# Attention and MoE on one core: sums of weights in three stages on VectorE, four buffers for the plain chunks' results, and visits of the first chunk 7 slots apart

## The chip, the core and the metric

The kernel runs on one core of a Trainium2 chip. The metric is the device time of one execution in microseconds (us); lower is better. A core has TensorE (PE in the profile; its weight loads are PEld), VectorE (DVE), ScalarE (ACT), GpSimd (POOL) and SyncE (SP). Each of these engines works through its own queue in order, so an instruction that waits holds up all that stand behind it on the same engine. DMAs are issued here from SP's, ScalarE's and GpSimd's queues.

## The reference

Windowed attention over 8 batches, 8 heads, 576 positions and head size 64, then a gated feed-forward layer on the 4608 resulting tokens:

```python
scores = scale * np.matmul(q, k.transpose(0, 1, 3, 2))
scores = np.where(masks, scores, -1e9)          # 32 keys back, plain or every 4th
attn = softmax(scores)                          # rows
x = (attn @ v).transpose(0, 2, 1, 3).reshape(4608, 512)
g = x @ w_gate                                  # 512 x 1536
out = (g * sigmoid(g) * (x @ w_val)) @ w_out    # 1536 x 512
```

Everything is float32 in and out.

## The kernel before

The tokens are cut into 12 chunks of 384 (`CH`). Float32 products are made of three products of a high and a low part in a format that TensorE takes fast (fp32r), so each operand is split: ScalarE copies it rounded (high), and another engine subtracts (low).

**Plain chunks.** The first four chunks are computed straight, in 48 steps `s` (loop at L757), 12 for each chunk, one for each 128 rows of the hidden layer. In a step TensorE runs three groups of 12 matmuls: gate into `bank_g` (`gv_mm`, L401), value into `bank_v` (L401), and out of the step before into the four banks `bank_o` (`out_mm`, L439). Between them ScalarE takes the tanh of the gate (`act_tanh`, L411), VectorE makes u and h (L416, L421), ScalarE and GpSimd split h (`h_hi` L426, `h_lo` L431). There is one bank for the gate, so u of a step must have been made before the gate group of the next step can start. Tanh, u and h live in two buffers that take turns (`t_ring`). At a chunk's end `out_store` (L442) copies the four banks, two on ScalarE (L446) and two on VectorE (L448), and stores them from SP's queue (L449).

**Weights.** In chunk 0 the weights arrive as 24 raw units and are turned into high and low parts: ScalarE L205, VectorE L212 and L213 (768 columns), ScalarE L221, GpSimd L225.

**Mixes.** The last eight chunks are computed in four pairs by a scheme with 7 products in place of 8 (`gate_val`, `outs`, L704), which needs sums of weight blocks. In chunks 1 to 3 these are made in 18 mixes (`mix`, L577). A mix adds high and low parts to whole float32 blocks in `q_at` (VectorE L587), makes four sums of 256 columns (L592, L594 and L595 on VectorE, L593 on GpSimd), copies 1024 columns to high parts (ScalarE L598) and subtracts to get the low parts (GpSimd L599). The results lie in one of two buffers (`l_ring`) and go to DRAM in `mix_out` (L606, four stores of 256 KB); three more stores take plain parts (L570). GpSimd's queue reads all pieces back in the paired chunks (L636).

**Visits.** Attention for the chunks to come is put between these groups. It comes in packs `m`, four to a chunk. `visit` is a table of slots, three to a step: in visit A of pack m TensorE makes the results of pack m-1 (L339) and the scores of pack m (L299, in banks `two`), VectorE divides (L348 to L350) and subtracts maxima (L311 to L314), ScalarE takes the exponential (L319). In visit B TensorE transposes (L357 for results, L323 for weights), ScalarE copies (L329) and x of pack m-1 is split (ScalarE L376, VectorE L377) or copied (L381).

**Order.** The program is traced in the order of the loops, and a scheduler then places the instructions on each engine's queue by its own estimates, so neighbours can change places. `tc.issue_after` holds a block behind one instruction on the same engine.

## Time and profile before

| What | Value |
|---|---|
| three executions | 991.89, 992.1, 993.73 us |
| their median | 992.1 us |
| the profiled execution | 996.74 us |
| its span, first to last instruction | 994.8 us |
| mean granted TensorE clock in it | 0.977 of full speed |
| busy: PE, DVE, ACT, POOL | 952.6, 658.4, 397.3, 430.4 us |
| stages in the span | first attention to 30 us, chunk 0 to 123, chunks 1 to 3 to 409, pairs from there |

A row of a timeline reads: start in us, duration in us, engine, line, operation, out<-in, shapes, and in brackets how long the engine sat idle before it and what ended that. A row with a bar reads: shapes and count | busy us, mean ns of one | idle before it and its releasers. In a table of windows each engine has its busy time and its count of instructions, then come the granted clock, the busy share of the DMA engines and GB/s. A group of 12 matmuls starts a fixed time after the one before when nothing waits.

### The profile page before, as it was taken

What the parts mean: (1) busy time and instruction counts of PE and PEld (TensorE: products, weight loads), DVE (VectorE), ACT (ScalarE), POOL (GpSimd) and SP (SyncE); (2) the same over time, 40 slices, a digit from 0 to 9 for tenths busy, and PEclk for the clock granted to TensorE, in tenths of its full rate; (3) what the DMA queues carried; (4) which work ended last, traced back from release to release, by engine and by line L of the source; (5) the groups of instructions that cost most, each with busy time, mean ns of one, the idle gap of its engine ahead of it and who ended that gap; (6) DMA issues with size and microseconds to landing.
All of it is one profiled execution on the core that took longest, in us unless ns stands there. A gap on an engine that the chain in (4) does not pass through costs nothing.

```text
span 994.8 us, 23912 instructions
## 1 busy us (share of the span) xinstructions
PE 952.6 (96%) x9960; PEld 924.7 (93%) x9960; DVE 658.4 (66%) x1144; ACT 397.3 (40%) x776; POOL 430.4 (43%) x496
## 2 busy tenths in 40 slices
PE   5898999999999898989999999999999999999998
PEld 4787899998989798989999999999999999999998
DVE  5777744556664644467688668688668679476583
ACT  4564422232323222333446244456244456244352
POOL 1564524343332342234337434346434347444473
PEclk7798999999999899999999999999999999999999
DMA  9665444665675595278988998998898987988873
GB/s 371 246 222 175 143 138 136 219 198 178 225 230 181 174 321 186 86 240 277 298 275 271 302 309 252 281 288 272 305 305 251 289 258 244 307 254 254 247 237 130
DMA packets 86060, 238.12 MB, mean 239 GB/s; under 512 B 8768, under 2 KB 29120, under 8 KB 85952
## 3 DMA queue, kind: packets, MB, share of 16 engines
q0 software_dynamic: 36288, 132.14, 43.0%
q1 hardware_dynamic: 36848, 65.07, 18.5%
q10 hardware_dynamic: 12816, 39.38, 12.3%
q8 instruction: 79, 1.29, 0.5%
q14 instruction: 29, 0.24, 0.1%
HBM read 194.08 MB, written 42.47 MB: 238 GB/s over the span
## 4 chain that ended last, share of the span: by engine, by line
PE 73%; DVE 12%; DMA 4%; issue 4%; ACT 3%; POOL 3%; SPq 0%; ACTq 0%; POOLq 0%; DVEq 0%
PE bo L704 29%; PE bg L704 11%; PE bv L704 11%; PE bg L401 6%; PE bo L439 5%; PE bv L401 5%; DMA out<-at_float 3%; DVE at_int L213 2%; PE two L339 2%; DVE at_int L212 2%; PE two L299 2%; POOL at_float32r L599 1%; DVE at_float32r L663 1%; PE two L323 1%; PE two L357 1%
## 5 line engine op out<-in xcount | busy, mean ns | idle before, releaser
L704 PE MATMUL bo<-at_float32r,at_float32r 128*128 128x384 f32 x1728 | 320.1, 337 | 3.5 <-DVE at_float L663 3.2
L704 PEld LDWEIGHTS bo<-at_float32r,at_float32r 128*128 128x128 f32 x1728 | 300.5, 188 | 5.2 <-DVE at_float L663 3.5
L636 POOL DMA_DIRECT2D at_float32r<-pieces x252 | 137.9, 547 | 237.4 <-PE bo L704 139.2
L663 DVE TENSOR_TENSOR at_float<-bo,at_float 128x384 f32<-128x384 f32 x224 | 121.7, 552 | 105.4 <-PE bo L704 52.5
L704 PE MATMUL bg<-at_float32r,at_float32r 128*128 128x384 f32 x648 | 137.0, 337 | 0.0
L704 PE MATMUL bv<-at_float32r,at_float32r 128*128 128x384 f32 x648 | 136.5, 336 | 0.0
L401 PE MATMUL bg<-at_float32r,at_float32r 128*128 128x384 f32 x576 | 117.3, 355 | 5.3 <-DVE at_float L416 4.1
L704 PEld LDWEIGHTS bv<-at_float32r,at_float32r 128*128 128x128 f32 x648 | 114.0, 188 | 0.5
L704 PEld LDWEIGHTS bg<-at_float32r,at_float32r 128*128 128x128 f32 x648 | 113.8, 188 | 0.7
L663 POOL TENSOR_TENSOR at_float32r<-at_float,at_float32r 128x384 fp32r<-128x384 f32 x84 | 91.8, 1093 | 51.9 <-ACT at_float32r L693 50.8
L401 PEld LDWEIGHTS bg<-at_float32r,at_float32r 128*128 128x128 f32 x576 | 107.1, 200 | 7.0 <-DVE at_float L416 4.7
L663 DVE TENSOR_TENSOR at_float32r<-at_float,at_float32r 128x384 fp32r<-128x384 f32 (+1 forms) x112 | 100.9, 923 | 18.6 <-ACT at_float32r L693 14.6
L439 PE MATMUL bo<-at_float32r,at_float32r 128*128 128x384 f32 x576 | 111.4, 341 | 1.5 <-POOL at_float32r L431 0.8
L431 POOL TENSOR_TENSOR at_float32r<-at_float,at_float32r 128x384 fp32r<-128x384 f32 x48 | 55.7, 1160 | 129.5 <-PE bo L439 80.6
L401 PE MATMUL bv<-at_float32r,at_float32r 128*128 128x384 f32 x576 | 110.7, 340 | 0.0
L693 ACT CAST at_float32r<-at_float 128x384 fp32r<-128x384 f32 x168 | 82.9, 512 | 63.8 <-PE bv L704 22.0
L439 PEld LDWEIGHTS bo<-at_float32r,at_float32r 128*128 128x128 f32 x576 | 100.9, 189 | 3.2 <-POOL at_float32r L431 1.6
L401 PEld LDWEIGHTS bv<-at_float32r,at_float32r 128*128 128x128 f32 x576 | 101.3, 189 | 0.8
L730 ACT ACTIVATE at_float<-at_float 128x384 f32<-128x384 f32 x96 | 50.6, 527 | 99.3 <-DVE at_float L663 94.4
L416 DVE SCALAR_TENSOR_TENSOR at_float<-at_float,bg 128x384 f32<-128x384 f32 x48 | 26.5, 553 | 77.3 <-ACT at_float L411 77.3
L663 DVE TENSOR_TENSOR at_float<-at_float,at_float 128x384 f32<-128x384 f32 (+1 forms) x64 | 54.6, 878 | 29.0 <-POOL at_float32r L663 11.3
L709 ACT COPY at_float<-bg 128x384 f32<-128x384 f32 x84 | 40.1, 477 | 80.1 <-PE bg L704 79.5
(75 smaller groups left out, 1033.6 us busy)
## 6 DMA issues: line engine op xcount, KB each, us to landing
at_float32r<-pieces POOLq DMA_DIRECT2D x252, 512.0 KB, 4.9
pieces<-at_float32r SPq DMA_DIRECT2D x126, 256.0 KB, 3.2
at_int<-w SPq DMA_DIRECT2D x24, 768.0 KB, 4.8
at_float<-vb ACTq DMA_DIRECT2D x36, 390.0 KB, 4.8
out<-at_float SPq DMA_DIRECT2D x48, 192.0 KB, 4.4
at_float<-qkb ACTq DMA_DIRECT2D x14, 448.0 KB, 5.6
at_float<-qkb ACTq DMA_DIRECT2D x15, 400.0 KB, 5.8
at_float<-qkb ACTq DMA_DIRECT2D x7, 640.0 KB, 6.0
```

The source lines that it names most:

```text
L212: nc.vector.tensor_scalar(out=y, in0=hi, scalar1=3, scalar2=None, op0=ALU.logical_shift_left)
L213: nc.vector.scalar_tensor_tensor(out=y, in0=lo, scalar=29, in1=y, op0=ALU.logical_shift_right, op1=ALU.bitwise_or)
L401: nc.tensor.matmul(out=bank[:, :CH], lhsT=wcol(f, o, low), rhs=x[k], start=n == 0, stop=n == 3 * NK - 1)
L416: last["h"] = nc.vector.scalar_tensor_tensor(out=t, in0=t, scalar=1.0, in1=bank_g[:, :CH], op0=ALU.add, op1=ALU.mult)
L431: nc.gpsimd.tensor_tensor(out=hl, in0=hst[i][0], in1=hst[i][1], op=ALU.subtract)
L439: nc.tensor.matmul(out=bank_o[j][:, :CH], lhsT=wcol(f, 2 * DM + P * j, low), rhs=x, start=f == 0 and n == 0, stop=f == NF - 1 and n == 2)
L636: nc.gpsimd.dma_start(out=taken[asked], in_=pieces[asked % NPIECE])
L663: engine.tensor_tensor(out=out, in0=a, in1=b, op=op)
L693: nc.scalar.copy(out=o[:, 0], in_=src)
L704: nc.tensor.matmul(out=bank, lhsT=w, rhs=x, start=first and n == 0 and t in FRESH, stop=last and n == len(ops) - 1, skip_group_check=True)
L709: nc.scalar.copy(out=kept[KEPT[t]][r], in_=banks[0][r][:, :CH])
L730: nc.scalar.activation(out=f, in_=g, func=AF.Tanh, scale=0.5)
```

## The change

It does three things. First, `out_store` has four buffers of 384 columns of its own at the end of the raw weights' area, which is free after chunk 0. Second, a mix is cut into three stages, `mix_parts`, `mix_sums` and `mix_low`, of which at most about one is traced in a half step (`mix_to`, called twice in a step), where before a whole mix was traced at the end of about every second step. All its arithmetic is on VectorE, apart from ScalarE's copy. There is one buffer for the results (`l_at`) in place of two, because the stores' buffers and the first paired inputs (`x32_first`, which leaves the spare area) need the room; another paired input (`x1_at`) moves from a mix buffer to the spare area. Third, the visits of packs 4 to 8 stand at slots 2 + 7n and 5 + 7n + 1, not 10 + 5n and 13 + 5n. The core of the diff:

```diff
-    x32_first = [at(o, 2 * CH).rearrange("p (k c) -> p k c", k=2) for o in (M_RAW + PIECE, M_SPARE)]
+    x32_first = [at(M_RAW + PIECE + 2 * CH * a, 2 * CH).rearrange("p (k c) -> p k c", k=2) for a in range(2)]
...
-            ot = t_ring()
+            ot = at(M_RAW + 8 * WU - CH * (j + 1), CH)
...
-        visits(4 + n, 10 + 5 * n, 13 + 5 * n)
+        visits(4 + n, 2 + 7 * n, 5 + 7 * n + (n < 4))
...
-    l_ring = Ring(2 * PIECE, M_RAW + 2 * PIECE, M_RAW + 4 * PIECE)
+    l_at = at(M_RAW + PIECE + 4 * CH, 2 * PIECE, F32R).rearrange("p (n l c) -> p n l c", n=4, l=2)
...
         nc.vector.tensor_tensor(out=a22, in0=a21, in1=a22, op=ALU.add)
-        nc.gpsimd.tensor_tensor(out=a21, in0=a11, in1=a21, op=ALU.subtract)
+        nc.vector.tensor_tensor(out=a21, in0=a11, in1=a21, op=ALU.subtract)
         nc.vector.tensor_tensor(out=a11, in0=a22, in1=a11, op=ALU.subtract)
         nc.vector.tensor_tensor(out=a12, in0=a12, in1=a11, op=ALU.subtract)
-        s = q.rearrange("p f h c -> p (f h) c")
-        t = l_ring(dt=F32R).rearrange("p (n l c) -> p n l c", n=4, l=2)
-        nc.scalar.copy(out=t[:, :, 0], in_=s)
-        nc.gpsimd.tensor_tensor(out=t[:, :, 1], in0=s, in1=t[:, :, 0], op=ALU.subtract)
-        mst[n] = i, which, t.bitcast(F32)
+        nc.scalar.copy(out=l_at[:, :, 0], in_=q_at.rearrange("p (n c) -> p n c", n=4))
+
+    def mix_low(n):
+        nc.vector.tensor_tensor(out=l_at[:, :, 1], in0=q_at.rearrange("p (n c) -> p n c", n=4), in1=l_at[:, :, 0],
+                                op=ALU.subtract)
...
-    def mix_step():
+    def mix_stage():
         nonlocal mixed
-        n = mixed
+        n, stage = divmod(mixed, 3)
         mixed += 1
-        if 0 < n <= 3 * NP:
-            mix_out(n - 1)
         if n < 3 * NP:
 
+            with tc.issue_after(last["h"].ins):
+                (mix_parts, mix_sums, mix_low)[stage](n)
             with tc.issue_after(last["w"].ins):
-                plain_parts(*divmod(n, 3))
-            with tc.issue_after(last["h"].ins):
-                mix(n)
+                if stage == 0:
+                    plain_parts(*divmod(n, 3))
+                elif stage == 2:
+                    mix_out(n)
...
-    x1_at = [at(o, 2 * CH).rearrange("p (k c) -> p k c", k=2) for o in (M_RAW + 2 * PIECE, M_XT)]
+    x1_at = [at(o, 2 * CH).rearrange("p (k c) -> p k c", k=2) for o in (M_SPARE, M_XT)]
...
+    def mix_to(half):
+
+        while mixed < half * 9 * NP // 62:
+            mix_stage()
...
         dve_u(s)
+        mix_to(2 * (s - NF) + 1)
...
-        if s >= NF and (s - NF) * 3 * NP // 31 >= mixed:
-            mix_step()
+        mix_to(2 * (s - NF) + 2)
```

In the changed kernel the mix's parts are L591, its four sums L597 to L600, ScalarE's copy L601, the low part L604, its stores L612, the plain stores L569, the pieces' reads L643, the subtraction of the pairs L670.

On VectorE, one mix of chunk 2 before: `at_1024` is `q_at`, `two` the banks of a visit, and the 8-column names belong to the division of a visit.

```order
L587 TENSOR_TENSOR at_1024_float_479<-at_1536_float32r 128x512 x2
L592 TENSOR_TENSOR at_1024_float_479<-at_1024_float_479 128x256
L348 TENSOR_SCALAR at_8_float_913<-two 128x8
L594 TENSOR_TENSOR at_1024_float_479<-at_1024_float_479 128x256
L349 RECIPROCAL at_8_float_913<-at_8_float_913 128x8
L595 TENSOR_TENSOR at_1024_float_479<-at_1024_float_479 128x256
L350 TENSOR_TENSOR at_512_float_914<-two,at_8_float_913 128x2x4x64
L311 TENSOR_TENSOR at_384_float_918<-two,at_352_bfloat_58 128x2x3x64
L313 TENSOR_REDUCE at_6_float_223<-at_384_float_918 128x6
L314 TENSOR_TENSOR at_384_float_918<-at_384_float_918,at_6_float_223 128x2x3x64
L416 SCALAR_TENSOR_TENSOR at_384_float_548<-at_384_float_548,bg 128x384
```

The same place of the changed kernel, where the mix is one stage earlier and the visit's rows follow behind these:

```order
L597 TENSOR_TENSOR at_1024_float_479<-at_1024_float_479 128x256
L598 TENSOR_TENSOR at_1024_float_479<-at_1024_float_479 128x256
L599 TENSOR_TENSOR at_1024_float_479<-at_1024_float_479 128x256
L421 SCALAR_TENSOR_TENSOR at_384_float_549<-at_384_float_549,bv 128x384
L600 TENSOR_TENSOR at_1024_float_479<-at_1024_float_479 128x256
L604 TENSOR_TENSOR at_2048_float32r<-at_1024_float_479,at_2048_float32r 128x4x256
L377 TENSOR_TENSOR at_384_float32r<-two,at_384_float32r 128x384
L416 SCALAR_TENSOR_TENSOR at_384_float_635<-at_384_float_635,bg 128x384
L421 SCALAR_TENSOR_TENSOR at_384_float_635<-at_384_float_635,bv 128x384
L591 TENSOR_TENSOR at_1024_float_479<-at_1536_float32r 128x512 x2
L348 TENSOR_SCALAR at_8_float_808<-two 128x8
```

The sums are no longer mixed with the rows of a visit; the low part (L604), which was GpSimd's, stands right behind the last sum and ahead of the x split (L377) and of the next u (L416).

On ScalarE, the end of chunk 2 before (names with addresses: 9024 and 9408 are the two buffers of `t_ring`):

```order
L411 ACTIVATE at9024_384_float32_548<-bg_471 128x384
L666 CAST at20160_768_float32r_480<-at11968_768_float32_106 128x768
L446 COPY at9408_384_float32_592<-bo0_473 128x384
L426 CAST at9792_384_float32r_570<-at9024_384_float32_548 128x384
L446 COPY at9408_384_float32_592<-bo2_475 128x384
L281 DMA at1928_780_float32_922<-vb 128x780
L275 DMA at648_1280_float32_477<-qkb 128x800
L411 ACTIVATE at9408_384_float32_592<-bg_471 128x384
```

The same place of the changed kernel:

```order
L411 ACTIVATE at9024_384_float32_549<-bg_471 128x384
L673 CAST at20160_768_float32r_481<-at11968_768_float32_106 128x768
L446 COPY at16704_384_float32_1528<-bo0_473 128x384
L426 CAST at9792_384_float32r_571<-at9024_384_float32_549 128x384
L446 COPY at15936_384_float32_1534<-bo2_475 128x384
L411 ACTIVATE at9408_384_float32_635<-bg_471 128x384
L281 DMA at1928_780_float32_817<-vb 128x780
L275 DMA at648_1280_float32_477<-qkb 128x800
L601 CAST at13504_2048_float32r_480<-at10944_1024_float32_479 128x4x256
```

The copies of the banks (L446) write to 16704 and 15936, and the next tanh (L411) has a buffer that no store reads.

On TensorE, from the first scores of chunk 0 (L299, pack 4) to their transposes (L323) before; this is between the value and out groups of step 3 and of step 4:

```order
L299 MATMUL two<-at_1280_float_477 32x64 x32
L439 MATMUL bo_473<-at_384_float32r,at_1536_float32r 128x384 x3
L439 MATMUL bo_474<-at_384_float32r,at_1536_float32r 128x384 x3
L439 MATMUL bo_475<-at_384_float32r,at_1536_float32r 128x384 x3
L439 MATMUL bo_476<-at_384_float32r,at_1536_float32r 128x384 x3
L401 MATMUL bg<-at_384_float32r,at_1536_float32r 128x384 x12
L401 MATMUL bv<-at_384_float32r,at_1536_float32r 128x384 x12
L323 MATMUL two<-at_256_float_59,at_512_float_755 128x128 x4
```

In the changed kernel, in step 2:

```order
L401 MATMUL bg<-at_384_float32r,at_1536_float32r 128x384 x9
L299 MATMUL two<-at_1280_float_477 32x64 x32
L401 MATMUL bg<-at_384_float32r,at_1536_float32r 128x384 x3
L401 MATMUL bv<-at_384_float32r,at_1536_float32r 128x384 x11
L323 MATMUL two<-at_256_float_59,at_512_float_613 128x128 x4
L401 MATMUL bv<-at_384_float32r,at_1536_float32r 128x384
```

The first pack's scores stand a step earlier than before, inside a gate group of step 2, with 14 matmuls between them and their transposes in place of 36; the packs behind it have four groups there in place of three, and three in place of two from their transposes to the next results.

More of the change, by code (lines that the diff above doesn't have):

```diff
@@ L573, in attention_moe, with halves, mix_parts @@
     q_at = at(M_RAW, PIECE)
-    l_ring = Ring(2 * PIECE, M_RAW + 2 * PIECE, M_RAW + 4 * PIECE)
-    mst = {}
-    def mix(n):
+    l_at = at(M_RAW + PIECE + 4 * CH, 2 * PIECE, F32R).rearrange("p (n l c) -> p n l c", n=4, l=2)
+    def halves(n):
+        q = q_at.rearrange("p (f h c) -> p f h c", f=2, h=2)
+        a, b, c, d = [q[:, f, h] for f in range(2) for h in range(2)]
+        return (a, b, c, d) if n % 3 < 2 else (a, c, b, d)
+    def mix_parts(n):
         i, which = divmod(n, 3)
@@ L588, in mix, with mix_sums @@
                 h += k
[L589 to L590 removed]
+    def mix_sums(n):
+        a11, a12, a21, a22 = halves(n)
         nc.vector.tensor_tensor(out=a22, in0=a21, in1=a22, op=ALU.add)
[L593 removed]
+        nc.vector.tensor_tensor(out=a21, in0=a11, in1=a21, op=ALU.subtract)
         nc.vector.tensor_tensor(out=a11, in0=a22, in1=a11, op=ALU.subtract)
         nc.vector.tensor_tensor(out=a12, in0=a12, in1=a11, op=ALU.subtract)
[L596 to L600 removed]
+        nc.scalar.copy(out=l_at[:, :, 0], in_=q_at.rearrange("p (n c) -> p n c", n=4))
+    def mix_low(n):
+        nc.vector.tensor_tensor(out=l_at[:, :, 1], in0=q_at.rearrange("p (n c) -> p n c", n=4), in1=l_at[:, :, 0],
+                                op=ALU.subtract)
     def mix_out(n):
[L603 removed]
+        i, which = divmod(n, 3)
+        t = l_at.bitcast(F32)
         for k, product in enumerate((2, 6, 4, 3) if which < 2 else (2, 4, 6, 3)):
```

3 lines of the change are left out of this document (removed).

## The prediction

> **What bounds the kernel now.** I first read the table of stages, cut where the plain chunks begin, where chunk 1 begins, where the paired chunks begin and where the start of those is over.
>
> ```profile
> core 0: us, PE busy (x) PEld busy (x) DVE busy (x) ACT busy (x) POOL busy (x), PEclk, DMA share, GB/s
> 29.90:122.77 92.87, 84.23 (x913) 79.28 (x914) 70.00 (x88) 47.42 (x74) 52.84 (x31) 0.94 0.58 189
> 122.77:409.35 286.58, 273.88 (x3040) 265.61 (x3040) 157.24 (x298) 84.18 (x155) 100.74 (x83) 0.98 0.57 190
> 409.35:431.24 21.89, 18.37 (x188) 17.29 (x187) 6.56 (x15) 5.56 (x12) 4.71 (x8) 0.92 0.53 172
> 431.24:980.00 548.76, 548.70 (x5322) 539.81 (x5321) 403.06 (x705) 244.85 (x512) 265.71 (x367) 1.00 0.88 273
> ```
>
> TensorE sets the time everywhere: from 431 us on it is never idle, so whatever is saved before moves the end by as much, and nothing later can be gained. The idle time that the change can reach is 92.87 - 84.23 = 8.64 us in chunk 0, 286.58 - 273.88 = 12.70 us in chunks 1 to 3, and 3.52 us at the start of the paired chunks. The clock column adds a part, worked out below. So I went through TensorE's timeline for the single idles, and looked at what each waited for.
>
> **Part one, the out buffers.** Before, the four copies of a finished chunk go through the two buffers that the tanh of the next steps uses.
>
> ```profile
> 229.95 2.35 PE L401 MATMUL bg<-at_float32r,at_float32r 128*128 128x384 f32 x12 [0.44 <-DVE at_float L416]
> 326.07 0.79 PE L439 MATMUL bo<-at_float32r,at_float32r 128*128 128x384 f32 x3 [0.68 <-DVE at_float L448]
> 329.16 0.49 ACT L411 ACTIVATE at_float<-bg 128x384 f32<-128x384 f32 x1 [6.09 <-DMA out<-at_float]
> 329.68 0.55 DVE L416 SCALAR_TENSOR_TENSOR at_float<-at_float,bg 128x384 f32<-128x384 f32 x1 [1.72 <-ACT at_float L411]
> 330.29 4.21 PE L401 MATMUL bg<-at_float32r,at_float32r 128*128 128x384 f32 x12 [3.42 <-DVE at_float L416]
> 427.57 0.56 DVE L663 TENSOR_TENSOR at_float<-bo,at_float 128x384 f32<-128x384 f32 x1 [5.16 <-DMA out<-at_float]
> 428.18 2.29 PE L704 MATMUL bo<-at_float32r,at_float32r 128*128 128x384 f32 x6 [3.19 <-DVE at_float L663]
> ```
>
> At 329 the tanh waited 6.09 us for a store to leave its buffer, and TensorE 3.42 us for what follows the tanh. At 428 the first paired sums waited for the same two buffers. With four buffers that nothing else touches in this time, all four waits go: 0.44 + 0.68 + 3.42 + 3.19 = 7.73 us. The idle has a tail. The gate group of 12 matmuls at 330 took 4.21 us, the one at 229.95 took 2.35: 1.9 us. The clock shows it:
>
> ```profile
> 283.20:286.40 3.20, 3.20 (x15) 3.20 (x14) 1.11 (x2) 1.35 (x4) 0.00 (x0) 0.67 1.06 398
> 330.20:334.30 4.10, 4.01 (x13) 3.91 (x13) 3.28 (x6) 1.03 (x2) 2.04 (x2) 0.50 0.00 0
> ```
>
> Six matmuls are half a group, 2.35 / 2 = 1.2 us; at 428 they took 2.29, so 1.1 us. Together 10.7 us. The copies and the stores stand where they stood, on SP's queue together ahead of the next mix's stores, and no wait is added: the new buffers' last readers are raw weights of chunk 0, later the stores of the chunk before. Bounds 8 (a wait of some 0.7 us stays at each of four chunk ends) and 10.7; I take 10, near the upper end, as the waits name the store and nothing else.
>
> **Part two, the sums of weights.** Before, GpSimd does one sum and the long subtraction.
>
> ```profile
> L599 POOL TENSOR_TENSOR at_float32r<-at_float,at_float32r 128x1024 fp32r<-128x1024 f32 x18 | 43.1, 2392 | 35.3 <-ACT at_float32r L598 31.6 <-DMA pieces<-at_float32r 2.1 <-PE bo L439 1.6
> 279.58 2.35 POOL L599 TENSOR_TENSOR at_float32r<-at_float,at_float32r 128x1024 fp32r<-128x1024 f32 x1 [1.95 <-ACT at_float32r L598]
> 280.07 2.28 DVE L314 TENSOR_TENSOR at_float<-at_float,at_float 128x384 f32<-128x384 f32 x1
> 282.96 0.55 PE L323 MATMUL two<-at_float,at_float 128*128 128x128 f32 x3 [2.33 <-ACT at_float L319]
> 283.26 3.34 PE L439 MATMUL bo<-at_float32r,at_float32r 128*128 128x384 f32 x12
> L314 DVE TENSOR_TENSOR at_float<-at_float,at_float x40: 547/557/2414, 121.4 to 812.0; 128x384 f32<-128x384 f32 x34, 128x512 f32<-128x512 f32 x6
> ```
>
> This is the mechanism I build on. VectorE's subtraction of the maxima (L314), 0.56 us in the median, takes 2.28 us here: it starts while GpSimd's long subtraction (L599) runs, from 279.58 to 281.93, and ends 0.42 us after it, as if it had done its work only then. The exponential and TensorE's transposes wait behind it. The same picture returns:
>
> ```profile
> 377.25 2.41 DVE L314 TENSOR_TENSOR at_float<-at_float,at_float 128x384 f32<-128x384 f32 x1
> 380.27 0.90 PE L323 MATMUL two<-at_float,at_float 128*128 128x128 f32 x3 [3.04 <-ACT at_float L319]
> 380.82 3.47 PE L401 MATMUL bg<-at_float32r,at_float32r 128*128 128x384 f32 x12
> 300.27 0.66 PE L323 MATMUL two<-at_float,at_float 128*128 128x128 f32 x4 [0.89 <-ACT at_float L319]
> 237.71 0.55 PE L323 MATMUL two<-at_float,at_float 128*128 128x128 f32 x3 [0.92 <-ACT at_float L319]
> ```
>
> Idle 2.33 + 3.04 + 0.89 + 0.92 = 7.2 us, slow groups 3.34 - 2.35 and 3.47 - 2.35 = 2.1 us: 9.3 us at stake.
>
> The Trainium skill (TensorE: Matmul & The Clock Gate, Part 1) lets the clock fall after an idle window of about 3.4 us. Here it fell to 0.67 after 2.33 us of idle, so the rows decide; by the page the 2.1 us here and the 1.1 us at 428 would not be owed to the idles, and the forecast would be some 3 us higher.
>
> What VectorE takes on: per mix one more sum of 256 columns and the subtraction of 1024.
>
> ```profile
> L594 DVE TENSOR_TENSOR at_float<-at_float 128x256 f32<-128x256 f32 x18 | 9.2, 513 | 19.1 <-POOL at_float L593 19.0
> 371.84 1.77 DVE L663 TENSOR_TENSOR at_float32r<-at_float,at_float32r 128x768 fp32r<-128x768 f32 x1
> 401.71 0.95 DVE L663 TENSOR_TENSOR at_float32r<-at_float,at_float32r 128x768 fp32r<-128x768 f32 x1
> L598 ACT CAST at_float32r<-at_float 128x1024 fp32r<-128x1024 f32 x18 | 18.9, 1049 | 56.1 <-DVE at_float L595 36.4 <-POOL at_float L593 8.7 <-DMA at_float<-qkb 4.2
> 36.55 2.24 PE L401 MATMUL bg<-at_float32r,at_float32r 128*128 128x384 f32 x12
> 38.63 2.24 PE L401 MATMUL bv<-at_float32r,at_float32r 128*128 128x384 f32 x12
> 369.29 0.96 DVE L663 TENSOR_TENSOR at_float<-at_float,at_float 128x768 f32<-128x768 f32 x1 [3.87 <-DMA pieces<-at_float32r]
> ```
>
> 768 columns took 0.95 us free and 1.77 us beside GpSimd, so 1024 is an estimate of 1.25 to 2.4 us, and I take 1.3, since GpSimd keeps only its short h_lo (L431). Per mix 0.5 + 1.3 = 1.8 us, for 18 mixes 32 us: VectorE goes from 157 to 189 us of 287, with room. In return its 19.0 us of waits for GpSimd's sum go, and with the first paired inputs in the spare area the 3.87 us that VectorE waited for a mix's stores at 369; TensorE did not idle there, so I count nothing. On the path this costs nothing as long as the step's u (L416) comes in time: a value and an out group lie between one gate group and the next, at 38.63 - 36.55 = 2.08 us each, 4.2 us, and tanh and u need 0.49 + 0.55 and two hand-overs, by my estimate 1.3 us: 2.9 us of slack. The low part waits for ScalarE's copy (1.05 us) and blocks what stands behind it in VectorE's queue, in the order shown above L377 and the next u: 1.05 + 1.3 = 2.4 us, inside the slack but not by much. Hence I take 7 of the 9.3 us; bounds 9.3 and 0, and below nothing by the rival on the buffer.
>
> **Part three, the visits of chunk 0.**
>
> ```profile
> 64.12 0.66 PE L323 MATMUL two<-at_float,at_float 128*128 128x128 f32 x4 [1.93 <-ACT at_float L319]
> 77.95 0.66 PE L357 MATMUL two<-at_float,at_float 128*128 128x128 f32 x4 [0.50 <-DVE at_float L314]
> 87.08 0.98 PE L339 MATMUL two<-at_float,at_float 64*32 64x65 f32 x48 [3.84 <-DVE at_float32r L377]
> 89.64 3.95 PE L401 MATMUL bg<-at_float32r,at_float32r 128*128 128x384 f32 x12
> 117.37 0.67 PE L339 MATMUL two<-at_float,at_float 64*32 64x65 f32 x44 [1.58 <-DVE at_float32r L377]
> ```
>
> All four idles come of VectorE's part of a visit (once through ScalarE's exponential, L319), which stands in its queue behind the bit work on the weights (L212, L213): 1.93 + 0.50 + 3.84 + 1.58 = 7.85 us, and 3.95 - 2.35 = 1.6 us of slow group: 9.5 us. By the order, scores to transposes and transposes to the next results get one more matmul group (2.08 us) from the second pack on. That covers 0.50 and 1.58 whole and about half of the 3.84 with its tail. The first pack is not helped: its transposes stand only 14 matmuls (2.4 us) behind its scores, and the reduction, subtraction and exponential need about 2 us once VectorE is free, so the 1.93 stays, perhaps larger by 0.5. Gain 0.50 + 1.58 + 1.9 + 1.6 - 0.5 = 5 us. Upper bound 9.5. Lower bound -2: VectorE is busy 70.00 of 92.87 us here, and the waits may only move with the visits.
>
> **Sum.** 10 + 7 + 5 = 22 us. The profiled execution took 996.74 us, its span 994.8: by it the change gives 974.7. The median of the runs shown is 992.1, 4.6 us less; I take this as the profile's own and keep the 22: 970.
>
> **The rivals.**
>
> *ScalarE's copy waits for the stores (slower).* One buffer now holds the mixed pieces, before two took turns. The copy of the next mix must wait until the four stores of the last one have landed, and the tanh stands behind it in ScalarE's queue.
>
> ```profile
> 338.89 1.79 SPq L606 DMA_DIRECT2D pieces<-at_float32r  x4
> 340.72 2.04 SPq L570 DMA_DIRECT2D pieces<-at_float32r  x3
> DMA to landing us min/median/max: 2.0/2.9/7.2
> ```
>
> The fourth issue comes 1.35 us behind the first, so the last landing is 4.3 us after the low part in the median and 8.6 in the worst. Low part to next copy is two stages, a step of 287 / 36 = 8.0 us less or more; in the tightest place of the order about 6 us. So typical landings are hidden and the worst are 2.5 us late. If all 17 were, and nothing hid it, that is 42 us: 970 + 42 = 1012. It decides from 22 / 17 = 1.3 us a mix on. For it speaks that seven stores follow in a row (four of the mix, three of plain parts); against it that DMA is busy only 0.57 of these stages.
>
> *VectorE becomes the late one.* The 32 us stand before the same subtraction that GpSimd held up; if they cost as much there, part two gives nothing and 977 remains. For it speaks that the low part with its wait, 2.4 us, is as long as the block was; against it that VectorE will be busy 189 of 287 us, and that the order puts the low part behind the visit's subtraction or a step away from it. The Trainium skill (Perfetto Trace Analysis, Optimizing Scalar/DVE Operations) has this rival as its rule: moving work between VectorE and GpSimd might not help, as they share a read port. The trace of before shows the sharing, but not the exchange.
>
> *All of it goes.* 10.7 + 9.3 + 9.5 = 29.5: 962.5. Against it stands the first pack of chunk 0.
>
> *The visits give nothing,* because the scheduler puts the first pack's scores into step 2, not step 0 as the numbers say: 975, inside the forecast's range.
>
> **The numbers.** The forecast (a gain of 15 to 27 us) 0.65; all of it 0.09; VectorE late or parts one or three halved, a gain of 8 to 15, 0.15; a gain of 2 to 8, 0.02; no change 0.04; slower by ScalarE's wait 0.05. A measurement can tell about 0.2% (2 us) here. Faster 0.91, same 0.04, slower 0.05. The range 963 to 983 goes from the sum of the upper bounds to nearly half of the forecast gain and leaves out some 0.17.
>
> **What would show it.** Right: no idle of TensorE that names L416 at 326 to 331 or L663 at 428; L314 never near 2.3 us in chunks 1 to 3; idle of chunks 1 to 3 under 6 us and of chunk 0 under 6. Wrong: ScalarE waiting for pieces' DMA ahead of its copy, tanh behind it; low parts near 2.4 us; TensorE idle for L377 or L319 as often as before, elsewhere.

## The result, and the profile after

The changed kernel takes 968.35 us in the median of four runs (967.49 to 970.3), the kernel before 992.75 us (991.89 to 993.73): a ratio of 0.9757, 95% interval 0.9737 to 0.9776, a gain of 24.4 us where 22 were forecast. The profiled executions are further apart: 996.74 us before (span 994.8), 967.76 us now (span 965.9), 28.9 us by the spans.

This is the table of stages of the changed kernel, cut at the same four groups of matmuls as before: the first gate group, the gate group of chunk 0's last step (which the prediction took as the start of chunk 1), the first paired group, and the end of the start of the pairs. The last row begins where the fourth stage ends.

```profile
core 0: us, PE busy (x) PEld busy (x) DVE busy (x) ACT busy (x) POOL busy (x), PEclk, DMA share, GB/s
30.70:119.08 88.38, 82.80 (x913) 77.47 (x914) 68.84 (x86) 46.18 (x72) 51.42 (x31) 0.97 0.57 197
119.08:385.89 266.81, 266.81 (x3039) 260.74 (x3039) 174.00 (x337) 85.60 (x157) 46.88 (x47) 1.00 0.60 204
385.89:402.36 16.47, 16.47 (x188) 16.09 (x187) 7.88 (x18) 6.08 (x13) 4.76 (x7) 1.00 0.75 235
402.36:951.00 548.64, 548.58 (x5321) 539.70 (x5320) 402.28 (x702) 244.69 (x511) 265.45 (x367) 1.00 0.87 273
```

Look at the second and third rows: TensorE is busy for the whole of both, where it had idled 12.70 and 3.52 us, and its clock is 1.00 in place of 0.98 and 0.92. Chunk 0 went from 92.87 to 88.38 us (4.49 less), chunks 1 to 3 from 286.58 to 266.81 (19.77 less), the start of the pairs from 21.89 to 16.47 (5.42 less). What follows is as long as it was: 994.8 - 431.24 = 563.56 before, 965.9 - 402.36 = 563.54 now. The first attention, which the change does not touch, was 0.8 us longer. 4.49 + 19.77 + 5.42 - 0.8 is 28.9 us, the whole difference of the two profiles. It is one pair of profiles: a second profile of each kernel (before_again and after_again below) gives 994.6 - 967.7 = 26.9 us, and the part that changed most is chunk 0, where that pair differs by 0.55 us and not by 4.49.

All of TensorE's waits in chunk 0 that are left, from its timeline (the last number is the idle before the row):

```profile
50.49 0.66 PE L323 MATMUL two<-at_float,at_float 128*128 128x128 f32 x4 [1.16 <-ACT at_float L319]
73.92 0.73 PE L339 MATMUL two<-at_float,at_float 64*32 64x65 f32 x48 [1.14 <-DVE at_float32r L377]
82.83 2.03 PE L439 MATMUL bo<-at_float32r,at_float32r 128*128 128x384 f32 x10 [0.26 <-POOL at_float32r L431]
91.84 2.03 PE L439 MATMUL bo<-at_float32r,at_float32r 128*128 128x384 f32 x10 [1.20 <-POOL at_float32r L431]
109.65 2.00 PE L439 MATMUL bo<-at_float32r,at_float32r 128*128 128x384 f32 x10 [1.74 <-POOL at_float32r L431]
```

The waits for the split of x (L377) fell from 5.4 to 1.14 us, the one for the first exponential (L319) from 1.93 to 1.16. But 3.2 us now name GpSimd's low part of h (L431), where 0.8 did before. The forecast had no term for these.

The low part of a mix in the groups by line and shape:

```profile
L604 DVE TENSOR_TENSOR at_float32r<-at_float,at_float32r 128x1024 fp32r<-128x1024 f32 x18 | 23.5, 1304 | 7.3 <-ACT at_float32r L601 7.3
```

The visit's subtraction in chunks 1 to 3 (shortest, median and longest in ns):

```profile
L314 DVE TENSOR_TENSOR at_float<-at_float,at_float x17: 549/557/1247, 119.9 to 368.3; 128x384 f32<-128x384 f32 x15, 128x512 f32<-128x512 f32 x2
```

And, from the waits, what ScalarE's copy into the single buffer waited for (us in total, times, longest; one more wait, of 0.7 us, names VectorE too):

```profile
ACT at_float32r L601 <- DVE at_float L600: 18.9, 12, 2.3
```

The low part takes 1.3 us as estimated (2.39 on GpSimd), the subtraction stays under 1.3 us, and the copy waits for the sums, never for a store.

### The profile page after: what moved, and what is told of

Same layout as the page of the kernel before. It is cut to its first block, busy times and chain, and to the rows that moved or that the text cites. A ratio compares the mean times of both kernels' runs of the same rounds, so it can differ in the third digit from the quotient of the medians.

```text
span 965.9 us, 23932 instructions
## 1 busy us (share of the span) xinstructions
PE 944.2 (98%) x9960; PEld 918.2 (95%) x9960; DVE 674.7 (70%) x1180; ACT 397.8 (41%) x776; POOL 374.9 (39%) x460
## 4 chain that ended last, share of the span: by engine, by line
PE 87%; DVE 7%; issue 3%; DMA 2%; ACT 1%; POOL 1%; ACTq 0%; POOLq 0%; SPq 0%
PE bo L711 30%; PE bg L711 11%; PE bv L711 11%; PE bg L401 9%; PE bo L439 9%; PE bv L401 8%; PE two L339 3%; PE two L299 2%; DVE at_int L213 2%; DVE at_int L212 2%; PE two L323 1%; PE two L357 1%; DMA at_int<-w 1%; DVE at_float32r L670 1%; DMA at_float<-qkb 1%
## 5 line engine op out<-in xcount | busy, mean ns | idle before, releaser
L643 POOL DMA_DIRECT2D at_float32r<-pieces x252 | 137.8, 547 | 242.0 <-PE bo L711 139.6
L670 DVE TENSOR_TENSOR at_float<-bo,at_float 128x384 f32<-128x384 f32 x224 | 122.1, 552 | 101.6 <-PE bo L711 52.0
L431 POOL TENSOR_TENSOR at_float32r<-at_float,at_float32r 128x384 fp32r<-128x384 f32 x48 | 57.6, 1200 | 214.7 <-PE bo L439 173.9
L711 PE MATMUL bg<-at_float32r,at_float32r 128*128 128x384 f32 x648 | 137.0, 336 | 0.0
L711 PEld LDWEIGHTS bg<-at_float32r,at_float32r 128*128 128x128 f32 x648 | 113.8, 188 | 0.7
L401 PE MATMUL bg<-at_float32r,at_float32r 128*128 128x384 f32 x576 | 112.5, 344 | 1.2 <-DVE at_float32r L390 1.2
L670 DVE TENSOR_TENSOR at_float32r<-at_float,at_float32r 128x384 fp32r<-128x384 f32 (+1 forms) x112 | 99.9, 915 | 17.9 <-ACT at_float32r L700 14.0
L670 POOL TENSOR_TENSOR at_float32r<-at_float,at_float32r 128x384 fp32r<-128x384 f32 x84 | 91.6, 1091 | 44.1 <-ACT at_float32r L700 43.1
L401 PEld LDWEIGHTS bg<-at_float32r,at_float32r 128*128 128x128 f32 x576 | 102.0, 191 | 2.9 <-DVE at_float32r L390 1.6
L416 DVE SCALAR_TENSOR_TENSOR at_float<-at_float,bg 128x384 f32<-128x384 f32 x48 | 26.6, 553 | 74.3 <-ACT at_float L411 74.3
L670 DVE TENSOR_TENSOR at_float<-at_float,at_float 128x384 f32<-128x384 f32 (+1 forms) x64 | 54.6, 878 | 25.0 <-POOL at_float32r L670 11.3
```

Of the source, the lines that this page charges most:

```text
L401: nc.tensor.matmul(out=bank[:, :CH], lhsT=wcol(f, o, low), rhs=x[k], start=n == 0, stop=n == 3 * NK - 1)
L416: last["h"] = nc.vector.scalar_tensor_tensor(out=t, in0=t, scalar=1.0, in1=bank_g[:, :CH], op0=ALU.add, op1=ALU.mult)
L431: nc.gpsimd.tensor_tensor(out=hl, in0=hst[i][0], in1=hst[i][1], op=ALU.subtract)
L643: nc.gpsimd.dma_start(out=taken[asked], in_=pieces[asked % NPIECE])
L670: engine.tensor_tensor(out=out, in0=a, in1=b, op=op)
L711: nc.tensor.matmul(out=bank, lhsT=w, rhs=x, start=first and n == 0 and t in FRESH, stop=last and n == len(ops) - 1, skip_group_check=True)
```

## The experiments

The kernels ran in three sets (the order of the texts below is another), each set beside runs of the kernel before on its chip. That kernel took 995.88, 996.56 and 996.26 us in the medians of the three sets, so ratios, and the stages of the profiles, are what is compared. The stages, all in us, with the two steps at the end of chunk 2 (the 330 us of the prediction) taken out of chunks 1 to 3:

| kernel | chunk 0 | chunks 1 to 3, rest | end of chunk 2 | start of pairs |
|---|---|---|---|---|
| before | 92.87 | 264.95 | 21.63 | 21.89 |
| before_again | 90.83 | 266.96 | 20.76 | 21.84 |
| changed | 88.38 | 252.18 | 14.63 | 16.47 |
| after_again | 90.28 | 252.35 | 14.65 | 16.50 |
| out_shared | 90.24 | 253.02 | 20.18 | 23.05 |
| old_visits | 91.16 | 252.18 | 14.63 | 16.47 |
| sums_on_gpsimd | 88.37 | 252.18 | 14.83 | 16.47 |
| vector_alone | 91.55 | 257.10 | 16.24 | 23.76 |
| stages_alone | 90.35 | 256.90 | 17.34 | 22.01 |
| visits_alone | 87.16 | 266.02 | 20.93 | 21.35 |
| wlow_on_vector | 93.09 | 252.35 | 14.65 | 16.50 |
| hlo_on_vector | 90.04 | 252.35 | 14.66 | 16.49 |
| first_b_later | 89.18 | 252.19 | 14.63 | 16.46 |
| visits_at_3 | 86.42 | 252.20 | 14.64 | 16.47 |

Each is the difference of two starts of groups in the timeline of that kernel's profile. One profile is one execution: the two of the kernel before differ by 2.0 us in chunk 0 and in the rest of chunks 1 to 3, the two of the changed kernel by 1.9 us in chunk 0 and by 0.2 us in the rest.

### The kernel before, a second profile (before_again)

Nothing edited.

> The kernel before, unchanged, profiled a second time. The first profiled execution took 996.74 us, 4 us above the median of the unprofiled runs. Theory A (the 4 us belong to that one execution): 991 to 994 us, the same idles of TensorE in the same places to 0.3 us, and what is shorter is the busy time, by a higher granted clock (0.98 or more in place of 0.977). Theory B (the profile of this kernel always costs 4 us): 996 to 997.5 us again.

Measured: 996.57 us, with the runs without a profile beside it at 995.88 (993.78 to 1000.2, 11 runs). The idles are the same in place and nearly in size; the wait for L377 in chunk 0 is 2.79 us in place of 3.84, the one at the end of chunk 2 is 2.41 in place of 3.42. So neither theory holds as written: 996.6 us came again, as theory B says, but the runs without a profile take as long here, so on this chip the profile costs nothing. Without a profile the kernel before takes 996 us here and took 992 to 993 beside the first result.

### Out buffers put back (out_shared)

```diff
-            ot = at(M_RAW + 8 * WU - CH * (j + 1), CH)
+            ot = t_ring()
```

> The changed kernel with the finished chunk's copies back in the two buffers of the tanh. Theory A (the waits name the stores, so the buffers alone decide): the 10 us come back, 976 to 980 us; TensorE waits for L416 or L448 at two of the three chunk ends, 3 us or more in all, and for the pairs' subtraction (L670) at the start of the pairs, about 3 us. Theory B (the stores were late only because a whole mix's stores and parts stood around them, which the stages have spread): under 4 us come back, below 972.

Measured: 983.4 us (980.05 to 986.42), ratio 0.9868 (0.9842 to 0.9894). From its timeline, ScalarE, VectorE and TensorE at the end of chunk 2 and at the start of the pairs:

```profile
319.36 0.49 ACT L411 ACTIVATE at_float<-bg 128x384 f32<-128x384 f32 x1 [2.72 <-DMA out<-at_float]
319.88 0.56 DVE L416 SCALAR_TENSOR_TENSOR at_float<-at_float,bg 128x384 f32<-128x384 f32 x1 [3.80 <-ACT at_float L411]
320.49 3.78 PE L401 MATMUL bg<-at_float32r,at_float32r 128*128 128x384 f32 x12 [3.25 <-DVE at_float L416]
...
405.18 3.25 PE L711 MATMUL bo<-at_float32r,at_float32r 128*128 128x384 f32 x12 [1.95 <-ACT at_float L446]
...
414.02 1.32 PE L711 MATMUL bo<-at_float32r,at_float32r 128*128 128x384 f32 x6 [1.78 <-DVE at_float L670]
```

The tanh waits for a store of the out again, then u, then TensorE, the same chain as before with shorter waits (2.72 us for the store, where it was 6.09). Theory A holds, and its amount was too small (976 to 980 us): the rest of chunks 1 to 3 is 0.84 us longer than in the changed kernel, the end of chunk 2 5.55, the start of the pairs 6.58, together 13.0 us. With the buffers shared, the end of chunk 2 takes 16.24 to 21.63 us in the six profiles of the table and the start of the pairs 21.35 to 23.76; with buffers of their own 14.63 to 14.83 and 16.46 to 16.50 in all eight. The two lowest of the six, vector_alone and stages_alone, show that the edits of part two shorten the end of chunk 2 as well, so the parts are not independent there.

### The sums and the low part back on GpSimd (sums_on_gpsimd)

```diff
-        nc.vector.tensor_tensor(out=a21, in0=a11, in1=a21, op=ALU.subtract)
+        nc.gpsimd.tensor_tensor(out=a21, in0=a11, in1=a21, op=ALU.subtract)
...
-        nc.vector.tensor_tensor(out=l_at[:, :, 1], in0=q_at.rearrange("p (n c) -> p n c", n=4), in1=l_at[:, :, 0],
+        nc.gpsimd.tensor_tensor(out=l_at[:, :, 1], in0=q_at.rearrange("p (n c) -> p n c", n=4), in1=l_at[:, :, 0],
```

> The changed kernel with its three stages, but the one sum (L598) and the low part (L604) on GpSimd as before. Theory A (VectorE is held up by GpSimd's long subtraction wherever the two meet): L314 or another operation of VectorE with two operands in memory takes 1.7 us or more in chunks 1 to 3, TensorE gets idles of 4 to 9 us there for L319 or L416, and the time is 972 to 977 us. Theory B (the stages alone did it, because the low part no longer starts at the visit's subtraction): idle of chunks 1 to 3 under 1.5 us, 967 to 970 us. Theory C (VectorE was near its limit with the 32 us): faster than the change, below 967.

Measured: 967.81 us (967.59 to 969.25), ratio 0.9714 (0.9693 to 0.9736). Its row of chunks 1 to 3 in the table of stages:

```profile
118.84:385.85 267.01, 267.01 (x3039) 260.73 (x3039) 152.42 (x301) 85.11 (x157) 100.94 (x83) 1.00 0.60 204
```

One visit of its timeline, from the scores to the transposes:

```profile
350.76 0.68 PE L299 MATMUL two<-at_float 64*32 64x64 f32 x44
...
351.48 0.17 DVE L348 TENSOR_SCALAR at_float<-two 128x6 f32<-128x6 f32 x1 [0.76 <-PE two L299]
...
352.75 2.40 POOL L604 TENSOR_TENSOR at_float32r<-at_float,at_float32r 128x1024 fp32r<-128x1024 f32 x1 [1.18 <-ACT at_float32r L601]
...
353.55 2.01 DVE L314 TENSOR_TENSOR at_float<-at_float,at_float 128x384 f32<-128x384 f32 x1
...
355.59 0.53 ACT L319 ACTIVATE at_float<-at_float 128x384 f32<-128x384 f32 x1 [1.31 <-DVE at_float L314]
...
358.15 0.49 PE L323 MATMUL two<-at_float,at_float 128*128 128x128 f32 x3
```

This is the row that the prediction built on, happening again: the subtraction takes 2.01 us beside GpSimd's 2.40 and ends 0.41 us behind it. Yet TensorE does not idle for one moment in chunks 1 to 3. The block is real, but beside the stages it costs no time. Theory B holds by its time and its idle; its reason does not, as the low part still runs into the visit's subtraction.

### Only the engine changed, mixes whole (vector_alone)

Made from the kernel before:

```diff
-        nc.gpsimd.tensor_tensor(out=a21, in0=a11, in1=a21, op=ALU.subtract)
+        nc.vector.tensor_tensor(out=a21, in0=a11, in1=a21, op=ALU.subtract)
...
-        nc.gpsimd.tensor_tensor(out=t[:, :, 1], in0=s, in1=t[:, :, 0], op=ALU.subtract)
+        nc.vector.tensor_tensor(out=t[:, :, 1], in0=s, in1=t[:, :, 0], op=ALU.subtract)
```

> The kernel before with one edit: the sum and the low part of a mix, L593 and L599, are on VectorE; mixes whole as before, buffers and visits as before. Theory A (GpSimd's long subtraction holding up VectorE is the cause): L314 is near 0.56 us everywhere, the mix idles of 7.2 us and their tails go, and the kernel is 7 to 9 us faster than before, ratio 0.991 to 0.993. Theory B (the place of the whole mix among a visit's rows is the cause): the visit's subtraction still comes 6 us or more after the scores, TensorE still waits 5 us or more for L319 in chunks 1 to 3, and the ratio is 0.997 to 1.008.

Measured: 985.12 us, ratio 0.9878 (0.9857 to 0.99). L314 is 0.55 to 0.69 us in all of chunks 1 to 3, and TensorE's waits for L319 fell from 7.2 to 2.9 us. Theory A holds for about three fifths of these waits. The kernel is faster than its 7 to 9 us all the same: 7.85 us go in the rest of chunks 1 to 3 and 5.39 more at the end of chunk 2, which the theory did not have. Why not all of the waits go, one visit of its timeline shows:

```profile
228.57 0.68 PE L299 MATMUL two<-at_float 64*32 64x64 f32 x44
...
229.47 2.24 DVE L587 TENSOR_TENSOR at_float<-at_float32r 128x256 f32<-128x256 f32 x4
...
233.01 0.16 DVE L348 TENSOR_SCALAR at_float<-two 128x6 f32<-128x6 f32 x1
...
235.21 1.22 DVE L599 TENSOR_TENSOR at_float32r<-at_float,at_float32r 128x1024 fp32r<-128x1024 f32 x1
236.35 0.55 DVE L314 TENSOR_TENSOR at_float<-at_float,at_float 128x384 f32<-128x384 f32 x1
...
236.93 0.52 ACT L319 ACTIVATE at_float<-at_float 128x384 f32<-128x384 f32 x1 [1.91 <-DVE at_float L314]
237.50 0.55 PE L323 MATMUL two<-at_float,at_float 128*128 128x128 f32 x3 [1.47 <-ACT at_float L319]
```

The scores are done at 229.25, but the whole mix stands in VectorE's queue around the visit's rows: its parts and three sums before L348, and the low part, 1.22 us, just where GpSimd's block had been. The rival of the prediction that VectorE becomes the late one is this row; here it costs 1.47 us, and in the changed kernel, with the stages, it is gone.

### Only the stages (stages_alone)

The changed kernel with the edits of out_shared, sums_on_gpsimd and old_visits together.

> The changed kernel with the out buffers, the visits and the engines of the sum and the low part all put back; what is left of the change is the three stages, the single buffer and the places of the first paired inputs. Theory A (the stages are part two): no idle over 0.4 us that names L319 or L377 in chunks 1 to 3, while those that name L416, L446, L448 and L670 stay; ratio 0.985 to 0.991. Theory B (the stages help only together with VectorE or the other parts): ratio above 0.994.

Measured: 983.38 us, ratio 0.9862 (0.9837 to 0.9888). L314 reaches 2.51 us. TensorE's waits from the end of chunk 0 to the pairs:

```profile
PE two L323 <- ACT at_float L319: 2.0, 4, 0.6
PE bg L401 <- DVE at_float L416: 1.7, 2, 1.2
PE bo L439 <- DVE at_float L448: 0.9, 1, 0.9
PE two L339 <- DVE at_float32r L377: 0.8, 2, 0.6
```

7.2 us for L319, one of 3.0, became 2.0 in four waits of up to 0.64. Theory A holds by the ratio and by the waits that stay, and misses its line of 0.4 us. The stages alone or the engine alone each save about 8 of the 12.8 us in the rest of chunks 1 to 3; in every kernel of the table with the stages and at least two of the other three parts (engine, buffers, visits), 11.9 to 12.8 go. Stages and engine are two cures for one wait, so their sizes don't add.

### The visits put back, and the visits alone (old_visits, visits_alone)

```diff
-        visits(4 + n, 2 + 7 * n, 5 + 7 * n + (n < 4))
+        visits(4 + n, 10 + 5 * n, 13 + 5 * n)
```

and the same edit the other way round in the kernel before. (As the diff has it, the second visit of the last of these packs stands at slot 33, without the 1.)

> The changed kernel with the visits of packs 4 to 8 back at 10 + 5n and 13 + 5n. Theory A (a longer distance hides VectorE's part of a visit): chunk 0 gets back idles of 0.5 to 3.9 us that name L377, 3 us or more in all, and the time is 971 to 974 us. Theory B (the waits only move with the visits): 967 to 970 us.

> The kernel before with one edit: the visits of packs 4 to 8 at 2 + 7n and 5 + 7n + 1. Putting the old visits back into the changed kernel cost 2.2 us of the median and 2.8 us in chunk 0 of the profile. Theory A (the visits' part stands by itself): 2 to 5 us faster than before, ratio 0.995 to 0.998, all of it in chunk 0. Theory B (it works only with the other parts, since later waits take up what the visits save): ratio 0.999 to 1.002.

Measured: old_visits 970.52 us, ratio 0.9737 (0.9715 to 0.9759), on another chip than the changed kernel's 0.9757, so its time does not tell them apart; visits_alone 994.86 us, ratio 0.9992 (0.9969 to 1.0014), where the runs scatter by 10 us. The times decide neither. Chunk 0 in the profiles does better: the five executions with the old visits (before, before_again, old_visits, vector_alone, stages_alone) take 90.35 to 92.87 us, mean 91.35, the five with the new ones (changed, after_again, out_shared, sums_on_gpsimd, visits_alone) 87.16 to 90.28, mean 88.89. That is 2.5 us, of which TensorE's idle is 1.9 (7.9 and 6.0 us in the mean). The margin is thin: the longest of the new ones and the shortest of the old ones are 0.07 us apart. TensorE's waits in chunk 0, of old_visits first:

```profile
PE two L339 <- DVE at_float32r L377: 4.7, 2, 3.1
PE two L323 <- ACT at_float L319: 1.9, 1, 1.9
...
PE bo L439 <- POOL at_float32r L431: 0.5, 1, 0.5
```

And of visits_alone:

```profile
PE bo L439 <- POOL at_float32r L431: 3.1, 4, 1.2
PE two L339 <- DVE at_float32r L377: 1.2, 1, 1.2
```

The wait for VectorE shrinks as forecast, and 2.3 to 2.7 us of it come back as waits for h's low part (0.8 before and 3.1 in visits_alone, 0.5 in old_visits and 3.2 in the changed kernel).

### What holds up h's low part in chunk 0 (hlo_on_vector, wlow_on_vector)

```diff
-        nc.gpsimd.tensor_tensor(out=hl, in0=hst[i][0], in1=hst[i][1], op=ALU.subtract)
+        (nc.vector if i < NF else nc.gpsimd).tensor_tensor(out=hl, in0=hst[i][0], in1=hst[i][1], op=ALU.subtract)
```

and, in another kernel, in `w_split_lo`:

```diff
-        nc.gpsimd.tensor_tensor(out=lo, in0=wst.pop(u).bitcast(F32), in1=hi, op=ALU.subtract)
+        nc.vector.tensor_tensor(out=lo, in0=wst.pop(u).bitcast(F32), in1=hi, op=ALU.subtract)
```

> The changed kernel with h_lo (L431) of the 12 steps of chunk 0 on VectorE, 0.55 us each, as it stands behind a weight's low part on GpSimd there. Theory A (GpSimd's queue is what h_lo waits for): the 3.2 us of waits for L431 go and nothing else moves, 964 to 967 us. Theory B (on VectorE it stands behind the bit work, L212 and L213, and is as late): 967 to 972 us, with TensorE waiting for L431 or L377 as long as before.

> The changed kernel with the low parts of the weights in chunk 0 (L225, 24 of 1.75 us on GpSimd) on VectorE too. The second operation on the bits (L213) takes 0.96 us alone and 2.15 to 2.27 us beside GpSimd. Theory A (the shared port costs VectorE as much as it gains): L213 falls to about 1.0 us on the mean and pays for much of the added 24 x 0.95 us, h_lo (L431) takes 1.0 us, the waits for L431 of 3.2 us in chunk 0 go: 964 to 967 us. Theory B (VectorE is the late one in chunk 0): L377, L416 and L319 come later, 969 to 980 us.

Measured: hlo_on_vector 969.14 us, ratio 0.9716 (0.9694 to 0.9739); TensorE waits 3.4 us for L431, now on VectorE, as long as before, and 2.0 for L319. wlow_on_vector 971.94 us, ratio 0.9744 (0.9719 to 0.977); chunk 0 takes 93.09 us. TensorE's waits there:

```profile
PE bg L401 <- DVE at_float L416: 6.7, 3, 4.2
```

And VectorE's bit work and low parts of the weights:

```profile
L213 DVE SCALAR_TENSOR_TENSOR at_int<-at_int,at_int 128x768 int32<-128x768 int32 x20 | 25.6, 1281 | 0.2
L225 DVE TENSOR_TENSOR at_float32r<-at_int,at_float32r 128x768 fp32r<-128x768 f32 x21 | 20.0, 951 | 5.1 <-ACT at_float32r L221 5.0
```

The mean of L213 fell from 1.54 to 1.28 us, 5.1 us in all, against 20.0 us added: the waits for L431 are gone, but u comes late, up to 4.2 us. Theory B holds for both by time and by waits. In chunk 0 neither move made the kernel faster: the wait went to another row.

### The changed kernel again, and two other places for the visits (after_again, first_b_later, visits_at_3)

```diff
-        visits(4 + n, 2 + 7 * n, 5 + 7 * n + (n < 4))
+        visits(4 + n, 2 + 7 * n, 5 + 7 * n + (n < 4) + 2 * (n < 1))
```

is first_b_later, and visits_at_3 is

```diff
-        visits(4 + n, 2 + 7 * n, 5 + 7 * n + (n < 4))
+        visits(4 + n, 3 + 7 * n, 7 + 7 * n)
```

> The changed kernel once more, on the chip of this set, with a profile of its own. Theory A: 967 to 969 us as the first time, the same idles to 0.3 us. On the chips of the two sets before, the kernel before took 995.9 and 996.6 us in place of 992.8, so the ratio may come out at 0.972, not 0.976: the kernel with the long idles is the one that differs from chip to chip, because what the clock does behind an idle differs. Theory B: the ratio stays at 0.976 and this kernel is slower here too, 971 us or more.

> The changed kernel with visit B of the first pack two slots later, so that its transposes stand behind the out group of the step, 24 matmuls behind the scores and not 14. Theory A (the 1.16 us of wait for L319 is the short distance): that wait goes, nothing else moves, 966 to 968 us. Theory B (the wait moves to the next results, L339, as only one group is left between the transposes and them): 967.5 to 971 us with an idle that names L377 or L329 at about 55 us.

> The changed kernel with the visits of packs 4 to 8 at 3 + 7n and 7 + 7n, a slot later: the same distance of 7, other places among the groups of a step. Theory A (the distance decides, not the place): 966 to 970 us, TensorE's idle in chunk 0 within 2 us of the 5.5 us of the changed kernel. Theory B (the place in the step decides, as h_lo and the bit work meet the visits at other points): idle in chunk 0 of 8 us or more, 971 us or more, or under 3 us.

Measured: after_again 970.31 us (967.72 to 972.93), ratio 0.9745 (0.9716 to 0.9773), between the two theories; five of its six idles are as the first time to 0.3 us, and one of 0.33 is new. first_b_later 968.16 us, ratio 0.9721 (0.9693 to 0.9748): the wait for L319 is gone and those for L431 grew from 3.2 to 4.5 us, so 5.5 us of idle are 5.5 us still, a third outcome that neither theory had. visits_at_3 966.33 us (965.7 to 967.68), ratio 0.9705 (0.9678 to 0.9733): every run lies below every run of the changed kernel in the same set, if only just. Theory A holds by its bounds. Its chunk 0 in the table of stages:

```profile
30.29:116.71 86.42, 81.58 (x913) 76.78 (x914) 68.49 (x86) 46.37 (x73) 52.82 (x31) 0.98 0.58 195
```

And TensorE's waits in it:

```profile
PE two L323 <- ACT at_float L319: 2.7, 2, 1.8
PE bo L439 <- POOL at_float32r L431: 0.9, 2, 0.5
```

4.84 us of idle, near the changed kernel's 5.58, but the waits for L431 are 0.9 us, so the place in the step decides which row is late. By its median it beats both kernels.

## Why the prediction was right, and where its sum was not

The sign, the time and the range held: 968.35 us against 970, within 963 to 983. The signs named in advance came in the first profile: no wait for L416 or L670 at a chunk's end, no long L314, idle in chunks 1 to 3 under 6 us (none), in chunk 0 under 6 (5.58; the second profile has 6.57). But that the time came within 2 us was partly luck: the sum falls short of the profiles' gain by 5 to 7 us, and within it parts one and two were too small where part three was too large.

**The basis.** "I take this as the profile's own and keep the 22." The 4.6 us between the profile and the median were taken as an accident of one execution. A second profile gave 996.57 and unprofiled runs in three other sets 996: the profile was a usual execution. Against its own time the forecast was 974.7 us, and the changed kernel's profile took 967.76. The gain is 28.9 and 26.9 us in the two pairs of profiles, 24.4 in the medians of the first result and 26.0 in those of the third set (996.26 and 970.31): the sum of 22 is too small by each of these, and nearest where the kernel before ran in 992.75.

**Part one, 10 us, bounds 8 to 10.7.** The mechanism was right; the term was too small, outside its bound. The end of chunk 2 gave 7.00 us and the start of the pairs 5.42, with 0.58 at the end of chunk 1: 13.0, and out_shared brought 13.0 back. The waits were read rightly (7.73 us, though one of 0.34 us for ScalarE's copy, L446, at 419.5 was left out); the tails were counted over one group of matmuls each, and lasted longer. The stage's row held it: of its 286.58 us TensorE was busy 273.88, 7 more than the 266.81 in which the same matmuls now run, and the sum had found 4.0 of these.

**Part two, 7 us, bounds 0 to 9.3.** 12.2 us went (about 14 against the second profile of the kernel before), outside the bound. By size: 7.2 us are the waits for L319 that the sum had, 1.0 three small waits that it left out, and the other 4.0 are slow groups, where it had counted 2.1; and it took only 7 of its 9.3. By mechanism, the step "This is the mechanism I build on" named one link of the chain as the cause, and the stages got no term of their own. In sums_on_gpsimd the same block, 2.01 us, costs nothing, and one of the four waits that the prediction listed as the same picture, 0.92 us at 237.71, had no block at all. The whole chain has to be measured, from the end of the scores to the exponential. Rows of the kernel before: the visit whose wait the prediction quoted at 282.96, one that did not wait, and the subtraction and exponential of the visit at 237.71:

```profile
273.05 0.69 PE L299 MATMUL two<-at_float 64*32 64x64 f32 x46
...
275.71 0.16 DVE L348 TENSOR_SCALAR at_float<-two 128x8 f32<-128x8 f32 x1
...
276.70 1.22 DVE L594 TENSOR_TENSOR at_float<-at_float 128x256 f32<-128x256 f32 x1 [0.84 <-POOL at_float L593]
...
282.38 0.52 ACT L319 ACTIVATE at_float<-at_float 128x384 f32<-128x384 f32 x1 [2.88 <-DVE at_float L314]
...
214.27 0.68 PE L299 MATMUL two<-at_float 64*32 64x64 f32 x44
...
218.58 2.03 DVE L314 TENSOR_TENSOR at_float<-at_float,at_float 128x384 f32<-128x384 f32 x1
...
220.65 0.53 ACT L319 ACTIVATE at_float<-at_float 128x384 f32<-128x384 f32 x1 [2.52 <-DVE at_float L314]
...
221.55 0.49 PE L323 MATMUL two<-at_float,at_float 128*128 128x128 f32 x3
...
236.56 0.55 DVE L314 TENSOR_TENSOR at_float<-at_float,at_float 128x384 f32<-128x384 f32 x1
...
237.14 0.52 ACT L319 ACTIVATE at_float<-at_float 128x384 f32<-128x384 f32 x1 [0.30 <-DVE at_float L314]
```

At 282 the exponential starts 8.6 us after the scores' end and TensorE waits 2.33; at 220 it starts 5.7 us after, behind a block of 2.03 us, and TensorE waits for nothing. At 237 it starts 7.6 us after its scores' end at 229.5, behind a subtraction of 0.55 us, and TensorE waits 0.92. In vector_alone it was 7.7 us and 1.47 of wait, in sums_on_gpsimd 4.2 and none. 8.6 - 2.33 and 7.7 - 1.47 both leave 6.2 to 6.3 us: that is the cover, about three groups of 2.08. It holds for the other visits too: in the profiles of before, vector_alone, stages_alone and sums_on_gpsimd, all eleven visits of chunks 1 to 3 at which TensorE waits for L319 start the exponential 6.4 us or more after the scores, none that starts it sooner makes TensorE wait, and start less wait is 6.1 to 6.8 us. A visit's own rows need 2.7 us, GpSimd's block adds 1.5 to 1.9, the mix's rows and the wait for GpSimd's sum, 0.84 us, the rest. The visit's rows and the block alone stay under the cover; with the mix's rows between them they pass it. So the block was a part of the cause: taking its excess over 0.56 us (2.28, 2.35 and 2.41 us at three of the four) off the waits leaves 2.7 of the 7.2 us, an estimate from these rows, and vector_alone, which takes the block away, left 2.9. The stages take most of the mix's rows away instead. That the gain needs the sums' move to VectorE, as the prediction assumed, the runs deny: alone it saves 7.85 us in the rest of chunks 1 to 3, the stages alone 8.05, and with the other parts there taking it back costs nothing (sums_on_gpsimd, 252.18 us as in the changed kernel).

**Part three, 5 us, bounds -2 to 9.5.** 2.5 us by the five and five executions. The terms of VectorE went as forecast or better (the first pack's 1.93 became 1.16, not 2.4). What failed is that the sum asked for what is late next only on VectorE: h's low part on GpSimd, 0.8 us of waits before, is 3.2 now. The lower bound's reason, that "the waits may only move with the visits", came true for about half of the term. Why h's low part is late then stays open: moved to VectorE it is as late (hlo_on_vector, 3.4 us), and with the visits a slot later 0.9.

**The rivals.** ScalarE's copy never waited for the stores, although the slowest landed 9.3 us after its issue (7.2 in the kernel before, from which the prediction had its 8.6 behind the low part): no copy names them, and one tanh, at 353.89, that names a store of pieces for 2.39 us starts 0.1 us after its gate group ends, and cost TensorE nothing. A place where it would bite was not tried. VectorE did not become the late one in chunks 1 to 3 (174.0 us busy of 266.81, where 189 were expected; L314 alone fell from 16.7 to 10.7 us in sum, with less work on GpSimd beside it). The Trainium skill (Perfetto Trace Analysis, Optimizing Scalar/DVE Operations) has it that a move between GpSimd and VectorE might not help; here one move did and three did not: 0.9878 for the mix in vector_alone, nothing once the stages were there, nothing for h's low part in hlo_on_vector, and a chunk 0 that is 2.8 us longer or more in wlow_on_vector.

## What to carry to other kernels

A wait is priced by the whole way from the work that starts it to the work that waits, against the cover that lies between; one slow row on that way is not the whole cause if the cover holds it elsewhere, so look for a place where the same row costs nothing, and for a wait without that row. Compare TensorE's busy time with the time that its matmuls need at full clock: the difference is the hidden price of a stage's idles, and here it was over a third of what chunks 1 to 3 gained. Where a stall is taken out, ask each engine in turn what is late next, and where two edits cure the same wait, don't add their gains.

## What the runs showed of the hardware

The same wait has different tails. Before the out group at about 109 us of chunk 0, TensorE idles 1.74 or 1.75 us in four profiles whose kernels are the same up to there, but for the first pack's visit in first_b_later. The window over the group behind it in the changed kernel:

```profile
109.65:111.49 1.84, 1.84 (x11) 1.84 (x12) 1.81 (x2) 0.00 (x0) 1.65 (x1) 1.00 0.00 0
```

The same window of after_again:

```profile
109.32:112.40 3.08, 3.08 (x10) 3.08 (x11) 3.05 (x4) 0.54 (x1) 1.64 (x1) 0.56 0.00 0
```

And the group's row in it:

```profile
109.32 3.29 PE L439 MATMUL bo<-at_float32r,at_float32r 128*128 128x384 f32 x10 [1.74 <-POOL at_float32r L431]
```

The ten matmuls took 2.00 us at clock 1.00 once, and 3.29, 3.44 (out_shared) and 3.21 us (first_b_later) at 0.53 to 0.58. This one group is 1.24 us of the 1.9 by which chunk 0 of the changed kernel's two profiles differs (88.38 and 90.28 us); their idles differ by 1.0, and 0.3 came back elsewhere. It may also be why the kernel before, which has many such idles, was spread over 991.74 to 1003.59 us in the third set (17 runs) while visits_at_3 was spread over 2 us (5 runs); that was not shown run by run. The Trainium skill (TensorE: Matmul & The Clock Gate, What's actually happening) lets the clock fall after an idle window of about 3.4 us of a free-running counter; the trace agrees in so far as the same idle brings it down in one execution and not in another, and differs in that 1.74 us can be enough.

The two engines slow each other in both directions. In chunk 0 of the changed kernel VectorE's second bit operation (L213), with two operands from memory, takes 0.96 us alone and 1.68 to 2.46 beside GpSimd's rows, and GpSimd's low part of h (L431) 1.00 us or, beside L213, up to 1.75. Not every row is held up: the first bit operation (L212), with one operand, takes 0.94 or 0.95 us all 20 times, also at 57.73 and 108.86, where a row of GpSimd runs all or nearly all the while. The long subtraction is 2.39 us on GpSimd and 1.30 in the mean on VectorE, so it holds up the rows behind it or beside it about half as long there.
